# A 128-byte tile at the upper edge of SBUF, in a kernel of linear attention and two MLPs

## The chip, the cores and the metric

The kernel runs on one core of a Trainium2 chip. The metric is the time of one execution on the device in microseconds (us), the median of several runs. The profile is of one execution; its times are counted from the first instruction, and its engines are TensorE (PE for matmuls, PEld for the loading of stationary operands), VectorE (DVE), ScalarE (ACT), GpSimd (POOL) and SyncE (SP).

## The reference

Attention with a feature map makes x of 2304 tokens by 512 features, and two MLPs with different activations follow, all in float32:

```python
q_p, k_p = (phi(q), phi(k))                     # exp(+-proj - max), 256 features
kv = np.einsum('bhsf,bhsd->bhfd', k_p, v)
num = np.einsum('bhsf,bhfd->bhsd', q_p, kv)     # and den; x = num / den
...
h = x @ w_in                                    # 512 -> 2048
g = h * np.cos(h)                               # first MLP
g = np.maximum(h, 0.0) + alpha * np.minimum(h, 0.0)   # second MLP
return (g @ w_out).astype(np.float32)           # 2048 -> 512
```

## The kernel before

**Three products for one.** In the MLPs every operand is split into a high and a low part of type float32r, and a product is the sum of three matmuls, high by high, high by low and low by high. `mm3` (L158 to L164) issues them in this order. All matmuls of both MLPs come from L163.

**A step.** The work of the MLPs is cut into 160 steps: 2 layers, 16 slices of 128 hidden features (`ft`), 5 groups of tokens (four of 512 and one of 256). In `moe_step` a step issues the first matmul of a later step (`hidden`, five steps ahead once the pipeline runs) and the second of its own (`output`), and in between what ACT, DVE and POOL have to do. The order on every engine is the one written out by hand.

- `hidden` is a run of 12 matmuls into a tile `ph`: 4 slices of the 512 features by 3 products. The moving operand is x (`xh`, `xl`), the stationary one is w_in (`wih`, `wil`). The run is 512 columns wide, or 256 in the small group.
- `activate` makes the gated tiles: `gh` is the high part (ACT, L85) and `gl` the low one (POOL, L86) of `r`.
- `output` in the first layer is a run of 12 matmuls into `po`, with the gated tiles as moving operand (512 or 256 columns) and w_out (`woh`, `wol`) as stationary one. In the second layer the roles are exchanged: w_out moves, always 512 columns, and slices of 128 columns of the gated tiles are stationary; a group of 512 tokens gives 12 matmuls, the small one 6.

So of the matmuls at L163 that are 512 columns wide, 1,536 write `ph`, 768 write `po` in the first layer and 864 write `po` in the second. In each layer 48 steps pair a 512-wide `ph` run with a 512-token `po` run, 16 pair a 256-wide `ph` run with a 512-token `po` run, and 16 pair a 512-wide `ph` run with the small group's `po` run, since `ph` is five steps ahead and the small group stays for at most four steps.

**Where the tiles lie.** Pools are taken from the lower end of SBUF upward or, with `side="right"`, from the upper end (229,344 bytes in a partition) downward. On the lower side lie `xh`, `xl`, the tiles of weights, `acc`, and the attention's `wk` and `qpp`; on the upper side lie `gp` (five buffers each of `gh` and `gl`) and `mt` (two of `r`), and before the MLPs the attention's `vp` (v) and `kw` (`kin`, `kp`). A tile of 128 x 512 numbers takes 2048 bytes of a partition. In the kernel before, `xh`, `xl` and all tiles of weights begin at 1888 modulo 2048, and all of `gh`, `gl` and `r` at 2016. Within a tile, the slices of x lie 9216 bytes apart (1024 modulo 2048, so that the four slices begin at 1888 and 864 in turn), and stationary slices of 128 columns lie 512 bytes apart.

Of the kernel before, what the change touches and what calls it, by code (L numbers as in the profile page):

```python
# [10 lines left out]
F32 = mybir.dt.float32  # L11
# [10 lines left out]
P = 128  # L22
# [6 lines left out]
def feature_map_attention_two_mlps(  # L29
# [30 lines left out]

    ctx.enter_context(tc.manual_schedule())

    const = ctx.enter_context(tc.tile_pool(name="const", bufs=1))
    small = ctx.enter_context(tc.tile_pool(name="small", bufs=2))
    xpool = ctx.enter_context(tc.tile_pool(name="xpool", bufs=1))
# [732 lines left out]
```

## Time and profile before

| | |
|---|---|
| time, median of 3 runs | 998.44 us (998.33 to 998.99) |
| profiled execution, first to last instruction (span) | 996.2 us |
| TensorE matmuls busy | 989.7 us, 99% of the span |
| DVE, POOL, ACT busy | 69%, 61%, 50% |
| share of PE in the chain that ended last | 96% |

The span leaves out what lies before the first and after the last instruction; 2.2 us lie between it and the median. No time of its own was taken for the profiled execution, so its span and these 2.2 us stand for it. Matmuls are pipelined: the record of one lasts about 0.39 us, while the next one starts about 0.23 us after it. What a matmul costs is read from start to start, or from a run of them in the chain.

### The profile page before, as it was taken

How to read it: one execution, taken by the hardware profiler on the slowest of the kernel's cores; microseconds unless marked ns; L12 is line 12 of the kernel's file. 1: busy time of each engine (PE TensorE's matmuls, PEld its weight loads, DVE VectorE, ACT ScalarE, POOL GpSimd, SP SyncE). 2: the span in 40 equal slices, each digit the busy share in tenths (PEclk: the TensorE clock that was granted, in tenths of full speed). 3: DMA queues.
4: the chain of work that ended last, by engine and by line, in shares of the span. 5: the costliest groups of instructions: out<-in, count | busy, mean ns of one | idle time of the engine just before them, and what ended most of it. 6: DMA issues, size and time to landing. Idle time of an engine off the chain costs nothing.

```text
span 996.2 us, 13997 instructions
## 1 busy us (share of the span) xinstructions
PE 989.7 (99%) x5145; PEld 838.6 (84%) x5145; DVE 686.3 (69%) x976; ACT 493.9 (50%) x967; POOL 606.4 (61%) x498
## 2 busy tenths in 40 slices
PE   9999999999999999999999999999999999999998
PEld 7999999888888888888888888888888888888886
DVE  6868686668886577647764789587748774875343
ACT  5888888866666476646665663132213221322100
POOL 3577787856667366536655889477537753775221
PEclk9999999999999999999999999999999999999999
DMA  6454543211111021101110111011101110110112
GB/s 166 108 149 120 151 126 91 71 44 60 64 43 64 22 63 44 43 22 62 44 43 22 43 59 48 22 62 45 43 22 58 50 43 22 50 55 1 43 58 91
DMA packets 64580, 60.63 MB, mean 61 GB/s; under 512 B 28928, under 2 KB 54656, under 8 KB 64512
## 3 DMA queue, kind: packets, MB, share of 16 engines
q1 hardware_dynamic: 64512, 59.75, 20.0%
q8 instruction: 40, 0.66, 0.3%
q14 instruction: 28, 0.23, 0.1%
HBM read 52.50 MB, written 4.79 MB: 58 GB/s over the span
## 4 chain that ended last, share of the span: by engine, by line
PE 96%; DVE 1%; ACT 1%; issue 1%; POOL 1%; POOLq 0%; ACTq 0%
PE ph L163 39%; PE po L163 39%; PE pj L453 6%; PE kv L494 5%; PE nm L578 5%; PE tp L534 2%; PE tp L430 0%; DVE acc L243 0%; ACT acc L553 0%; DVE wt L125 0%; DVE wt L122 0%; DVE we L126 0%; ACT qp1h L567 0%; POOL wol L133 0%; POOL gl L86 0%
## 5 line engine op out<-in xcount | busy, mean ns | idle before, releaser
L86 POOL TENSOR_TENSOR gl<-r,gh 128x512 fp32r<-128x512 f32 (+1 forms) x160 | 204.1, 1277 | 305.4 <-ACT gh L85 300.4
L85 ACT CAST gh<-r 128x512 fp32r<-128x512 f32 (+1 forms) x160 | 92.1, 576 | 392.9 <-DVE r L209 266.9
L163 PE MATMUL ph<-xh,wil 128*128 128x512 f32 (+1 forms) x640 | 236.7, 370 | 0.0
L163 PE MATMUL ph<-xh,wih 128*128 128x512 f32 (+1 forms) x640 | 236.5, 370 | 0.0
L163 PE MATMUL ph<-xl,wih 128*128 128x512 f32 (+1 forms) x640 | 236.0, 369 | 0.0
L243 DVE TENSOR_TENSOR acc<-po,acc 128x512 f32<-128x512 f32 (+1 forms) x134 | 86.9, 658 | 104.7 <-PE po L163 104.1
L163 PEld LDWEIGHTS ph<-xl,wih 128*128 128x128 f32 x640 | 120.5, 188 | 22.3 <-POOL xl L622 0.2
L163 PEld LDWEIGHTS ph<-xh,wih 128*128 128x128 f32 x640 | 120.5, 188 | 22.0
L163 PEld LDWEIGHTS ph<-xh,wil 128*128 128x128 f32 x640 | 120.4, 188 | 21.3
L163 PE MATMUL po<-gh,wol 128*128 128x512 f32 (+1 forms) x320 | 119.5, 373 | 0.1
L163 PE MATMUL po<-gh,woh 128*128 128x512 f32 (+1 forms) x320 | 119.0, 372 | 0.0
L163 PE MATMUL po<-gl,woh 128*128 128x512 f32 (+1 forms) x320 | 119.0, 372 | 0.0
L163 PE MATMUL po<-woh,gh 128*128 128x512 f32 x288 | 114.0, 396 | 0.0
L163 PE MATMUL po<-woh,gl 128*128 128x512 f32 x288 | 113.6, 394 | 0.1
L163 PE MATMUL po<-wol,gh 128*128 128x512 f32 x288 | 113.6, 395 | 0.0
L122 DVE SCALAR_TENSOR_TENSOR wt<-ws,we 128x512 int32<-128x512 int32 x64 | 97.9, 1530 | 2.4
L196 DVE TENSOR_SCALAR r<-ph,al 128x512 f32<-128x512 f32 (+1 forms) x80 | 55.3, 691 | 58.0 <-PE ph L163 38.1
L131 POOL TENSOR_TENSOR wu<-wu,we 128x512 f32<-128x512 f32 x64 | 83.0, 1297 | 1.3 <-ACT wu L128 1.3
L207 DVE TENSOR_TENSOR r<-ph,r 128x512 f32<-128x512 f32 (+1 forms) x80 | 50.5, 631 | 47.8 <-ACT r L194 47.7
L569 POOL TENSOR_TENSOR qp1l<-acc,qp1h 128x512 fp32r<-128x512 f32 (+1 forms) x64 | 59.1, 949 | 26.4 <-ACT qp1h L567 26.4
L494 PEld LDWEIGHTS kv<-vm,kp 128*128 128x128 f32 x512 | 72.3, 191 | 2.6 <-ACT qp1h L567 0.4
L494 PE MATMUL kv<-vm,kp 128*128 128x66 f32 x512 | 72.2, 255 | 0.1
(81 smaller groups left out, 1876.0 us busy)
## 6 DMA issues: line engine op xcount, KB each, us to landing
ws<-in_moe_w_in_dram SPq DMA_DIRECT2D x32, 512.0 KB, 3.6
ws<-in_moe_w_out_dram SPq DMA_DIRECT2D x32, 512.0 KB, 3.5
acc<-dr SPq DMA_DIRECT2D x32, 144.0 KB, 3.0
out_dram<-acc SPq DMA_DIRECT2D x18, 256.0 KB, 2.0
vm<-in_v_dram SPq DMA_DIRECT2D x16, 256.0 KB, 3.5
kin<-in_k_dram SPq DMA_DIRECT2D x28, 128.0 KB, 2.8
qin<-in_q_dram SPq DMA_DIRECT2D x28, 128.0 KB, 2.8
acc<-acc SPq DMA_DIRECT2D x16, 144.0 KB, 2.4
```

The costliest lines, as they stand in the source:

```text
L85: nc.scalar.copy(hi, src)
L86: lo_engine.tensor_tensor(out=lo, in0=src, in1=hi.bitcast(F32), op=ALU.subtract)
L122: lambda: stt(out=t, in0=w1, scalar=-0x40000000, in1=e, op0=ALU.bitwise_and, op1=ALU.bitwise_or),
L131: lambda: tt(out=u, in0=u, in1=ef, op=ALU.mult),
L163: nc.tensor.matmul(ps, lhsT=l, rhs=r, start=(first and m == 0), stop=(last and m == n - 1))
L196: nc.vector.tensor_scalar(out=r, in0=ph, scalar1=0.0, scalar2=al[:, ft:ft + 1], op0=ALU.min, op1=ALU.mult)
L207: nc.vector.tensor_tensor(out=r, in0=ph, in1=r, op=ALU.mult)
L243: nc.vector.tensor_tensor(out=a, in0=po, in1=a, op=ALU.add)
L453: nc.tensor.matmul(pj[:, a].rearrange("p j f -> p (j f)"), lhsT=x[:, a * P:(a + 1) * P], rhs=w2.rearrange("p j f -> p (j f)"), start=True, ...
L494: nc.tensor.matmul(ps[:, :, y, :] if pr is None else ps[:, pr, y, :], lhsT=e[:, s, 2 * a + y, :], rhs=vt[:, y] if pr is None else vm[:, pr ...
L569: nc.gpsimd.tensor_tensor(out=dl, in0=et, in1=dh.bitcast(F32), op=ALU.subtract)
L578: nc.tensor.matmul(nm, lhsT=l[:, s, pr, y * VW:(y + 1) * VW], rhs=r[:, s, y, :], start=(s == 0 and m == 0), stop=(s == 1 and m == 2),)
```

## The change

A pool of one tile of 128 x 32 float32 numbers (128 bytes in a partition) is taken at the upper edge of SBUF before any other pool, and no instruction uses it:

```diff
     ctx.enter_context(tc.manual_schedule())
 
+    edge = ctx.enter_context(tc.tile_pool(name="edge", bufs=1, side="right"))
+    edge.tile([P, 32], F32, name="edge")
     const = ctx.enter_context(tc.tile_pool(name="const", bufs=1))
```

All pools of the upper side begin 128 bytes lower: `gh`, `gl` and `r` at 1888 modulo 2048, like x and the weights, and `kin`, `kp` and v 128 bytes below their former places. The lower side stays where it is. No instruction is added, removed or moved.

## Rows read from the trace of the kernel before

**Rows 1.** The page's head and its engines' busy times.
```profile
span 996.2 us, 13997 instructions
...
PE 989.7 (99%) x5145; PEld 838.6 (84%) x5145; DVE 686.3 (69%) x976; ACT 493.9 (50%) x967; POOL 606.4 (61%) x498
```

**Rows 2.** The chain that ended last, by line, from the page.
```profile
PE ph L163 39%; PE po L163 39%; PE pj L453 6%; PE kv L494 5%; PE nm L578 5%; PE tp L534 2%; PE tp L430 0%; DVE acc L243 0%; ACT acc L553 0%; DVE wt L125 0%; DVE wt L122 0%; DVE we L126 0%; ACT qp1h L567 0%; POOL wol L133 0%; POOL gl L86 0%
```

**Rows 3.** Stretches: length, then busy us (count) of each engine, granted clock, DMA.
```profile
560.00:600.00 40.00, 40.00 (x181) 32.81 (x180) 33.67 (x41) 23.34 (x43) 34.61 (x27) 1.00 0.16 54
...
sum 996.20, PE 989.75 PEld 838.65 DVE 686.34 ACT 493.91 POOL 606.43; mean PE 39.59 PEld 33.55 DVE 27.45 ACT 19.76 POOL 24.26
```

**Rows 4.** Groups of instructions by form: one of each kind of 512-wide matmul.
```profile
L163 PE MATMUL ph<-xh,wih 128*128 128x512 f32 x512 | 200.5, 392 | 0.0
...
L163 PE MATMUL po<-woh,gh 128*128 128x512 f32 x288 | 114.0, 396 | 0.0
...
L163 PE MATMUL po<-gh,wol 128*128 128x512 f32 x256 | 101.3, 396 | 0.1
```

**Rows 5.** The chain's pieces at the first step: start, length, what, count.
```profile
196.88 10.90 PE ph L163 x48
```

**Rows 6.** PE in order of time: start and length of two matmuls, twelve apart.
```profile
204.90 0.39 PE L163 MATMUL ph<-xh,wih 128*128 128x512 f32 x1
...
207.62 0.40 PE L163 MATMUL po<-gh,woh 128*128 128x512 f32 x1
```

**Rows 7.** The chain's pieces in the first layer, 512-token groups.
```profile
480.71 2.79 PE po L163 x12
483.50 2.73 PE ph L163 x12
...
508.35 2.79 PE po L163 x12
```

**Rows 8.** The chain's pieces in the second layer, 512-token groups.
```profile
680.53 2.80 PE po L163 x12
683.32 2.76 PE ph L163 x12
...
708.29 2.80 PE po L163 x12
```

**Rows 9.** The chain's pieces in the first layer, `po` runs of the small group.
```profile
448.77 2.76 PE ph L163 x12
451.53 1.44 PE po L163 x12
...
461.37 2.76 PE ph L163 x12
```

**Rows 10.** The chain's pieces in the second layer, `po` runs of the small group.
```profile
648.76 2.73 PE ph L163 x12
651.49 1.40 PE po L163 x6
...
661.14 2.73 PE ph L163 x12
```

**Rows 11.** The chain's pieces near the end, `ph` run of the small group.
```profile
974.91 1.43 PE ph L163 x12
976.35 2.77 PE po L163 x12
...
983.39 4.63 issue
```

**Rows 12.** PE in order of time: the first `po` matmuls of the second layer.
```profile
608.19 0.40 PE L163 MATMUL po<-woh,gh 128*128 128x512 f32 x1
608.43 0.40 PE L163 MATMUL po<-wol,gh 128*128 128x512 f32 x1
```

**Rows 13.** Groups by form: the attention's projections from the lower and the upper side.
```profile
L453 PE MATMUL pj<-w,qin 128*128 128x256 f32 x126 | 33.1, 381 | 0.0
L453 PE MATMUL pj<-w,kin 128*128 128x256 f32 x126 | 33.0, 380 | 0.0
```

## The prediction

> **What bounds the kernel.** I read the page's head first, then the chain, then the stretches. PE is busy for 989.7 of 996.2 us [rows 1], and the chain that ended last runs on PE for 96% of its length, 78% of it in the two kinds of matmul at L163 [rows 2]. [...] So the time is the number of matmuls by the distance from one start to the next, and an edit that adds no instruction can only act through that distance.
>
> A record's length doesn't give it: ph and po records last 392 and 396 ns alike [rows 4], since they overlap. The chain does, because consecutive matmuls of one kind stand in it as one piece. Equal matmuls, 128 x 128 by 512 columns, go at different paces there. Twelve ph matmuls between two starts take 207.62 - 204.90 = 2.72 us [rows 6], and 48 in a row, before any po is mixed in, take 10.90 us, 0.227 us each [rows 5]. Twelve po take 2.79 us in the first layer [rows 7] and 2.80 in the second [rows 8], 0.233 each. The ph runs between them take 2.73 [rows 7] or 2.76 [rows 8]. There is no wait in it: idle time before these groups is 0.0 or 0.1 us in total [rows 4]. It is a pace, and I look for what sets it.
>
> **What differs between ph and po.** While one matmul streams its moving operand, the stationary operand of the next is loaded, so PE reads two places of SBUF at a time (PEld is busy for 84% of the span beside PE's 99% [rows 1]). In ph both places begin at 1888 modulo 2048 plus a multiple of 512 bytes (x at 1888 or 864, slices of w_in 512 apart). In po one of the two is a gated tile at 2016, so they are 128 bytes off that grid, in both layers, though the gated tile moves in the one and is stationary in the other. The slow pace goes with the offset and not with the role. In the twelve ph of rows 6 the four slices put the moving and the next stationary operand at distances of 0, 512, 1024 and 1536 modulo 2048, and none of these four is slower than the other three: 2.72 us over twelve. And ph runs are slower when they lie between po runs (2.73 and 2.76) than when they follow each other (2.72), which I read as a state that the po run leaves behind and that takes some matmuls to die out.
>
> **The change, part by part.** The new tile has no instruction, so it costs nothing by itself, and every engine keeps its program and its order. All of the upper side moves together by 128 bytes, so the tiles that overlap in it (gated tiles over the attention's) are the same ones and no wait between them is new. What is left is the distance between operands on the upper and on the lower side.
>
> *Matmuls at L163.* I take it that po on the grid of 512 goes as ph does, 2.72 us for a run of twelve, and that ph, with nothing off the grid beside it, stays at 2.72. By kinds of step, with the counts of the text above:
> - First layer, 48 full steps: five ph and po pairs take 508.35 - 480.71 = 27.64 us, 5.528 each [rows 7]; at 2 x 2.72 = 5.44 that is 0.088 less, 4.2 us.
> - Second layer, 48 full steps: (708.29 - 680.53) / 5 = 5.552 [rows 8], 0.112 less, 5.4 us.
> - First layer, 16 steps with the small group's po: (461.37 - 448.77) / 3 = 4.20, of which 1.44 are twelve po of 256 columns [rows 9]. Twelve ph of 256 columns take 1.43 [rows 11], so that width gains nothing or 0.01, and the ph run goes from 2.76 to 2.72: 0.04, 0.6 us.
> - Second layer, 16 such steps, with six po of 512 columns: (661.14 - 648.76) / 3 = 4.127 [rows 10]; at 2.72 + 1.36 = 4.08, 0.047 less, 0.75 us.
> - 32 steps with a small ph run and a full po run: 2.79 in the first layer [rows 7], 0.07 less, 1.1 us; 2.77 in the second [rows 11], 0.05 less, 0.8 us.
>
> The sum is 4.2 + 5.4 + 0.6 + 0.75 + 1.1 + 0.8 = 12.85 us.
>
> *What is given back.* A run of another width may leave a state behind too, even on the grid. This happens 48 times (32 small ph runs, 16 small po runs in the first layer). From below it costs nothing; from above it costs 0.04 us, which is what ph pays after a small po run today [rows 9], 1.9 us in all. The nearest row without an offset is the start of ph after the attention's last matmuls, which are of another width: 10.90 against 4 x 2.72 = 10.88, 0.02 us [rows 5]. I take that, 1.0 us. Near the end the chain leaves PE for 4.63 us [rows 11], so some 20 matmuls' gain of 0.006 us is lost, 0.1 us.
>
> *The attention.* kin, kp and v move against the operands of the lower side. The projections read the one (qin) from the lower and the other (kin) from the upper side, at different places modulo 2048, and last 381 and 380 ns [rows 13]: I take 0. For kv and nm, which are mixed matmul by matmul, no row tells; the chain gives them 10% of the span, 100 us [rows 2]. From both sides I allow 1 us, about what 1% of it would be.
>
> *The other engines.* They read and write the tiles at the same distances among themselves, since gh, gl and r move together. Faster steps press them harder: 5.54 to 5.44 us is 2%, so POOL's 34.61 of 40 [rows 3] becomes 88%, still with room. I cost that at nothing; with the room gone, PE would wait for gl, and the gain would shrink, not turn.
>
> So 12.85 - 1.0 - 0.1 = 11.75 us less. The span of 996.2 goes to 984.4 or so, and with the 2.2 us around it, or from the median at once, 998.44 - 11.75 = 986.7 us.
>
> [...]
>
> **The rivals.**
>
> *No change.* The pace follows something that the edit leaves alone. In ph the moving operand changes its place by 1024 from slice to slice and in po it stays in one tile or two, and po goes to other tiles. For it: no po run on the grid is in the trace. Against it: the two layers, with exchanged roles, have the same slow pace, and ph runs suffer from po as neighbours [rows 7, 8]. Time: 998.44, within 1 us by the attention.
>
> *Half of it.* The offset matters, but po on the grid doesn't stay in the even state; each change between ph and po costs as much as today in ph, and all runs take 2.73 to 2.76, 2.745 on average. Then a full pair takes 5.49: 48 x 0.038 + 48 x 0.062 = 4.8 us, and the small steps give some 1.5. Time: 992.1. For it: ph pays that today on either side of po. Against it: 48 ph in a row pay it once at most [rows 5].
>
> *Slower.* The same place modulo 2048 makes the two reads meet, not pass. The first products of every slice 0 have moving and stationary operand at distance 0; if po locks there at the slowest distance that the trace has, 608.43 - 608.19 = 0.24 us [rows 12], the 1,632 po of 512 columns take 0.007 us more each, 11 us. Time: 1009 to 1010. It decides from where a po run of twelve takes over 2.81 us: 2 us over 136 such runs is 0.015 on 2.795. For it: today's offset may be the luckier one of two, and nothing excludes that state for operands fixed in place. Against it: ph has distance 0 in a quarter of its matmuls and goes at 2.72 [rows 6].
>
> **How the numbers follow.** Full gain 0.61, half 0.16, no change 0.15, slower 0.08. The prediction is that of the full gain, 986.7; its own range is 984.7 (nothing given back, and 1 us from the attention) to 989 (all of 1.9 given back, 1 us lost in the attention, and runs at 2.725). The range for 8 in 10 reaches through the half case into the one of no change: 984.7 to 998.5, which leaves out most of the slower case, some of no change and a little below. Faster by over 0.2% (2 us, about what a measurement tells from nothing) is the full and the half case, 0.77; same 0.15; slower 0.08.
>
> **What would show it.** In the chain of the changed kernel, po runs of twelve at 2.72 in both layers, next to ph runs of 2.72; pairs of 5.44. Half the gain would show as 2.73 to 2.76 in both kinds. If po stays at 2.79 and 2.80, the place isn't the cause. If po takes 2.83 or more, they meet. If PE shows waits for gl or gh that aren't there now, another engine took over. I would be wrong most simply if the grid is not 512 bytes wide where one operand lies at the upper end of SBUF, which no row shows.

## The result and the profile after

987.69 us median (987.54 to 987.93) against 998.38 for the kernel before on the same chip: a ratio of 0.9888, 95% interval 0.9877 to 0.9900, 10.7 us less. Forecast were 986.7 us, 984.7 to 989 for the full gain and 984.7 to 998.5 for the range as a whole.

The page's head, against [rows 1]: the same instructions and a span 10.2 us shorter. PE's busy time is 11.6 us less (989.7 to 978.1), so PE is idle for 1.4 us more than before.

```profile
span 986.0 us, 13997 instructions
...
PE 978.1 (99%) x5145; PEld 838.0 (85%) x5145; DVE 688.5 (70%) x976; ACT 493.9 (50%) x967; POOL 606.5 (62%) x498
```

The chain's pieces of the changed kernel in the first layer (start, length, what, count), two line numbers further down than before. They answer to [rows 7].

```profile
481.27 2.72 PE ph L165 x12
483.99 2.72 PE po L165 x12
486.71 2.72 PE ph L165 x12
```

And in the second layer, against [rows 8]:

```profile
678.31 2.72 PE ph L165 x12
681.03 2.72 PE po L165 x12
683.75 2.72 PE ph L165 x12
```

Where 2.79 and 2.80 alternated with 2.73 and 2.76, every run of twelve beside others of its width takes 2.72, in both layers and in both kinds. A pair went from 5.53 and 5.55 to 5.44. The runs that are not at 2.72 stand behind a run of another width. In the chain, first the first layer, then the second, against [rows 9 to 11]:

```profile
449.69 1.43 PE po L165 x12
451.12 2.75 PE ph L165 x12
```
```profile
630.61 1.43 PE ph L165 x12
632.04 2.75 PE po L165 x12
...
642.95 1.36 PE po L165 x6
644.31 2.72 PE ph L165 x12
```

After twelve matmuls of 256 columns, the next run of 512 columns takes 2.75; after six po of 512 columns, it takes 2.72. PE in order of time shows where the 0.03 us go in such a run:

```profile
446.78 0.40 PE L165 MATMUL ph<-xh,wih 128*128 128x512 f32 x1
...
448.17 0.39 PE L165 MATMUL ph<-xh,wih 128*128 128x512 f32 x1
...
449.53 0.28 PE L165 MATMUL po<-gh,woh 128*128 128x256 f32 x1
```

The first six take 448.17 - 446.78 = 1.39 us, the last six 449.53 - 448.17 = 1.36, which is 0.227 each. So what the change of width leaves behind is gone after six matmuls when the operands are on the grid.

PE's waits on POOL in the changed kernel (waited for: us in total, times, longest us). In the kernel before, PE's matmuls have none, though its weight loads wait at the same two places:

```profile
PE ph L165 <- POOL xl L624: 0.3, 1, 0.3
PE po L165 <- POOL wol L135: 0.2, 1, 0.2
```

The weight loads there, before and after:

```profile
PEld po L163 <- POOL wol L133: 0.5, 1, 0.5
...
PEld ph L163 <- POOL xl L622: 0.2, 1, 0.2
```
```profile
PEld po L165 <- POOL wol L135: 0.7, 1, 0.7
PEld ph L165 <- POOL xl L624: 0.6, 1, 0.6
```

### The profile page after: what moved, and what is told of

Read it like the earlier page. It is cut to its first block, busy times and chain, and to the rows that moved or that the text cites. A ratio compares the mean times of both kernels' runs of the same rounds, so it can differ in the third digit from the quotient of the medians.

```text
span 986.0 us, 13997 instructions
## 1 busy us (share of the span) xinstructions
PE 978.1 (99%) x5145; PEld 838.0 (85%) x5145; DVE 688.5 (70%) x976; ACT 493.9 (50%) x967; POOL 606.5 (62%) x498
## 4 chain that ended last, share of the span: by engine, by line
PE 94%; ACT 2%; DVE 1%; issue 1%; DMA 1%; POOL 1%; SPq 0%; POOLq 0%; ACTq 0%
PE po L165 39%; PE ph L165 38%; PE pj L455 6%; PE kv L496 5%; PE nm L580 5%; PE tp L536 2%; DMA acc<-in_q_dram 0%; DMA dn<-acc 0%; ACT acc L555 0%; DVE r L192 0%; DVE wt L127 0%; ACT acc L593 0%; ACT r L195 0%; ACT r L184 0%; ACT r L196 0%
```

## The experiments

All place tiles of no use, as the change does, and nothing else, but for three that also shift x within a longer tile. "Distance" is the place of the moving operand minus that of the stationary operand of the next matmul, modulo 256, where all slices of x, of the weights and of the gated tiles fall together. The chain's pieces are given as above.

**Place or distance.** The tile at the lower end instead of the upper (x and weights join the gated tiles at 2016):

```diff
+    low = ctx.enter_context(tc.tile_pool(name="low", bufs=1))
+    low.tile([P, 32], F32, name="low")
     const = ctx.enter_context(tc.tile_pool(name="const", bufs=1))
```

> The tile of 128 bytes lies at the lower end instead of the upper: x and the weights go up to 2016 modulo 2048 and meet the gated tiles, which stay at 2016. If the distance between the two operands counts (my theory): as the changed kernel, 987.7 us, all runs of twelve at 2.72. If the place of the gated tiles itself counts (rival: 1888 is good, 2016 is bad at the upper end): as before, 998.4, po at 2.79 and 2.80.

Measured: 987.50 us, ratio 0.9896 (0.9882 to 0.9911), all runs of twelve beside others of their width at 2.72. Then the tile at both ends, this one and that of the change:

> A tile of 128 bytes at either end: the gated tiles lie at 1888 as in the changed kernel, x and the weights at 2016, so the distance of 128 bytes is back with the other sign. Distance theory: slow again, 998 us within 3, po at 2.77 to 2.83. Rival of the gated tiles' own place: 987.7, po at 2.72.

Measured: 998.67 us, ratio 1.0003 (0.9994 to 1.0013). The gated tiles lie where the changed kernel has them, and the slow pace is back; the second layer in the chain:

```profile
680.98 2.80 PE po L167 x12
683.78 2.76 PE ph L167 x12
```

So the distance counts and not the gated tiles' own place, and +128 and -128 go alike, po at 2.79 in the first layer and 2.80 in the second for both (with the period of 256 found below they are one and the same distance).

**The slow pace handed to ph.** The tile between x and the weights (x at 1888, everything else at 2016), none at the upper edge:

```diff
     xpool = ctx.enter_context(tc.tile_pool(name="xpool", bufs=1))
+    low = ctx.enter_context(tc.tile_pool(name="low", bufs=1))
+    low.tile([P, 32], F32, name="low")
```

> A tile of 128 bytes between x and the weights on the lower side, none at the upper edge: weights and gated tiles at 2016, x alone at 1888. Distance theory: po goes at 2.72 or is held up a little by its neighbours (up to 2.76), and ph takes over the slow pace, 2.77 to 2.83; 128 ph runs by 0.075 and 136 po runs by up to 0.025 make 9.6 to 13 us over the changed kernel, 997 to 1000 us. Rival that the slow pace is po's own (other tiles, the high part taken twice in a row from one place): po stays at 2.79 to 2.80 and ph gets no slower than 2.76.

Measured: 997.91 us, ratio 0.9998 (0.9988 to 1.0008). The total alone would say that nothing happened. The chain says that the two kinds changed places:

```profile
484.40 2.79 PE ph L165 x12
487.19 2.73 PE po L165 x12
489.93 2.79 PE ph L165 x12
```

The pace isn't po's own. The run on the grid takes 2.73 beside a neighbour off it, as ph did in the first layer before the change.

**The same place modulo what.** The upper tile with 640 bytes instead of 128, so that the gated tiles lie 512 bytes below the weights modulo 2048:

> The upper tile has 640 bytes instead of 128, so the gated tiles begin at 1376 modulo 2048, 512 bytes below the weights and x. If the grid is 512 bytes (my theory): 987.7 us, all runs at 2.72. If the same place modulo 2048 is what counts (rival): po slower than 2.73, the time above 989 and up to 998.

Measured: 987.75 us, ratio 0.9897 (0.9883 to 0.9912), all full runs at 2.72. The same place modulo 2048 isn't needed.

**Other distances.** The next runs change two sizes, the lower tile's (between x and the weights) and the upper one's. Here 256 and 1856 bytes:

```diff
+    edge = ctx.enter_context(tc.tile_pool(name="edge", bufs=1, side="right"))
+    edge.tile([P, 464], F32, name="edge")
...
+    low = ctx.enter_context(tc.tile_pool(name="low", bufs=1))
+    low.tile([P, 64], F32, name="low")
```

> Other distances modulo 2048: ph at 256 (weights 256 bytes above x), po at 64. Both signs of 128 gave the same sequence of paces, so I expect a period of 256: ph has its pace of 2.72 when it follows ph and 2.72 to 2.76 beside po. If the period is 512 (rival), ph at 256 differs from 2.72 also in the middle of a run. For po at 64: half way between 0 and 128 gives 2.755 and with ph at 2.735 about 994 us; a pace as even as at 0 gives 988.

Measured: 998.38 us, ratio 0.9998 (0.9989 to 1.0007); neither 994 nor 988. Pieces of the first layer, then of the second:

```profile
480.85 2.76 PE po L167 x12
483.62 2.77 PE ph L167 x12
```
```profile
680.68 2.80 PE po L167 x12
683.48 2.75 PE ph L167 x12
```

po differs by layer. The gated tiles lie 64 above the weights; in the first layer they move (distance +64, 2.76), in the second they are stationary (-64, 2.80). I had left the sign out. Lower 64 and upper 1856 bytes:

> The two distances exchanged: ph at 64, po at 256. Period of 256: po 2.72 to 2.76; ph at 64 as po was in the run with po at 64, since moving and stationary operands count alike. Time within 1.5 us of that run, since there are 128 runs of the one and 136 of the other. If po differs from ph at the same distance, the role or the tile counts after all (rival).

Measured: 997.53 us, ratio 0.9990 (0.9981 to 1.0000), 0.9 from the run before. ph, now at -64, takes 2.80, as po of the second layer did there. po at 256, in the chain and then matmul by matmul:

```profile
481.11 2.74 PE po L167 x12
483.85 2.80 PE ph L167 x12
```
```profile
480.94 0.39 PE L167 MATMUL po<-gh,woh 128*128 128x512 f32 x1
...
482.32 0.39 PE L167 MATMUL po<-gh,woh 128*128 128x512 f32 x1
...
483.68 0.39 PE L167 MATMUL ph<-xh,wih 128*128 128x512 f32 x1
```

Its first six matmuls take 1.38 us and its last six 1.36, the pace of the grid. So the grid is 256 bytes wide and not 512. Lower 32 bytes, no upper tile:

> Distances of 32 (ph) and 96 (po), no tile at the upper edge. If the pace grows with the distance from the grid, ph is near 2.74 and po near 2.78, 995 us. If it depends on whether both fall into one line of 64 or 128 bytes (rival), 32 is as 0 (2.72) or 96 is as 128 (2.79), in steps and not in proportion.

Measured: 1006.34 us, ratio 1.0078 (1.0063 to 1.0093), slower than before and 11 us above what I had. po at +96 and -96 takes 2.81, ph at -32 2.79 to 2.80. Nothing grows in proportion with the distance. Lower 192 and upper 1824 bytes:

> Distances of 192 (ph) and 160 (po), on the other side of 128. If the sign doesn't count (period 256), 192 is as 64 and 160 as 96 in the two runs before, run of twelve by run of twelve within 0.01 us. If it counts (rival), they differ; a distance at which a run takes under 2.72 would show here or in the three before.

Measured: 1000.30 us, ratio 1.0020 (1.0011 to 1.0030). The weights lie 192 above x, so ph's distance is -192, which is +64 modulo 256, and po's is -96 in the first layer and +96 in the second. First layer:

```profile
487.10 2.81 PE po L167 x12
489.92 2.75 PE ph L167 x12
```

The expectation that the sign doesn't count fell: 192 isn't as 64 in the run before (2.80). It is as +64 in the run with po at 64 (2.76): the period of 256 holds, with the sign.

**How exact it must be.** x was put 16, -16 and 8 bytes off by a slice in a longer tile (from number 4, 60 or 2 on; 60 numbers are 240 bytes, -16 modulo 256; the weights go up by 512 bytes and stay on the grid); the first kernel also has an upper tile of 96 bytes, the others of 128:

```diff
-    xh = xpool.tile([P, KD, NTOK], F32R, name="xh")
-    xl = xpool.tile([P, KD, NTOK], F32R, name="xl")
+    xh, xl = (
+        xpool.tile([P, KD * NTOK + 64], F32R, name=nm)[:, 4:4 + KD * NTOK].rearrange(
+            "p (k n) -> p k n", k=KD
+        )
+        for nm in ("xh", "xl")
+    )
```

> By the runs so far the pace depends on the moving operand's place minus that of the next stationary one, with its sign, modulo 256. Here that distance is +16 in ph, +32 in po of the first layer and -32 in po of the second. My theory from the earlier runs: the second layer's po at 2.79 to 2.80, as ph was at -32; +32 lies between 0 (2.72) and +64 (2.76) and gives up to 2.80; +16 at 2.72 if one line of 32 or 64 bytes is what has to agree, 2.75 or more if every byte counts (rival). 990 to 1000 us.

Measured: 1002.40 us, ratio 1.0034 (1.0021 to 1.0047); ph 2.78, po 2.80 in both layers. The time lies above the 990 to 1000 that I had: +16 isn't on the grid, and +32 is as slow as -32.

> ph at -16, po on the grid. If -16 is as slow as -32, ph at 2.79 and po at 2.74 beside it, 997 us; if it is within one line with 0, 987.7. A pace under 2.72 in the middle of a run would be new.

Measured: 997.61 us, ratio 0.9988 (0.9979 to 0.9997); ph 2.80, but po 2.72 beside it, where I had 2.74.

> ph at +8, po on the grid. If lines of 16 bytes or more are what count, as the changed kernel, 987.7 us and 2.72 everywhere; if every byte counts (rival), ph over 2.74 and 991 us or more.

Measured: 1000.95 us, ratio 1.0020 (1.0010 to 1.0030). Eight bytes are as bad as 128, and po on the grid beside them takes 2.75, where it took 2.73 with x 128 bytes off:

```profile
485.66 2.81 PE ph L169 x12
488.47 2.75 PE po L169 x12
```

**The MLPs' part alone.** The tile is taken when the attention's pools of the upper side are given back, so kin, kp and v stay where they were:

```diff
                 pctx.close()
+                edge = ctx.enter_context(tc.tile_pool(name="edge", bufs=1, side="right"))
+                edge.tile([P, 32], F32, name="edge")
                 pools["gp"]
```

> The tile of 128 bytes is taken only when the attention's upper pools are given back, so gh, gl and r move to 1888 as in the changed kernel while kin, kp and v stay where they were before. If the attention's places cost nothing (my prediction's step): 987.7 us within 0.5, all runs of the MLPs at 2.72. If moving them gave or took something (rival), the time differs from 987.7 by that, up to 1 us either way.

Measured: 987.53 us, ratio 0.9891 (0.9874 to 0.9907), all full runs at 2.72. The median is 0.2 from the changed kernel's, within the noise. The spans tell more: 984.9 to 985.5 us in its four executions, 985.8 to 986.0 in the changed kernel's four. So the attention's places do cost something; how much is worked out below.

## Why the prediction was right

**The bound.** PE's pace sets the time: the MLPs became shorter by the distance between starts (twelve po of 512 columns from 2.79 and 2.80 to 2.72), with the same 13,997 instructions.

**The cause.** The step from the rows to "128 bytes off the grid" held, and the rivals fell each on its own run. *No change*: exchanging which operand is off exchanges which run is slow. *Half of it*: all runs beside others of the same width are at 2.72, none at 2.73 to 2.76. *Slower*: distance 0 is not the slow one; for 512 columns, of the eleven distances tried (0, +8, +16, +32, +64, +96, 128, -96, -64, -32, -16) it has the best pace, 0.227 us, and 2.75 to 2.82 for twelve, beside runs of the same width, were measured at the others. The grid was called 512 bytes; it is 256, which changes nothing in the sum, since 128 is off both.

**The sum.** The full pairs came out as put down, 5.44 in both layers. In the MLPs, from the first ph run to the end, the stretch went from 996.2 - 188.19 = 808.0 to 986.0 - 188.86 = 797.1 us: 10.9 less, where 12.85 - 1.1 = 11.75 was forecast. The chains there: before, after, and in the kernel that leaves the attention's tiles in place:

```profile
188.19 2.77 PE ph L163 x12
```
```profile
188.86 2.75 PE ph L165 x12
```
```profile
188.23 2.76 PE ph L163 x12
```

Two terms of the MLPs were sized too small. What a change of width leaves behind is 0.027 us and not 0.02 (2.747 against 2.720, medians by the starts in the trace), 48 times 1.3 instead of 1.0 us. And "I cost that at nothing", of the other engines, left out that two weight loads already waited for POOL, for `xl` and for `wol`; these waits grew. The run of twelve at the first goes from 1.66 to 2.04 us, the one at the second from 3.10 to 3.31, though its pace alone makes it 0.05 shorter: 0.6 us together. With 0.1 for the end, which no run read by itself, that is 12.85 - 1.3 - 0.6 - 0.1 = 10.85. The chain shows the first of the two waits:

```profile
211.21 1.44 POOL xl L624
212.69 0.50 PE ph L165 x2
```

Only at the second does the faster pace explain the wait: counted from the first ph run, PE is there 1.2 us earlier and `wol` only 1.0. At the first PE is 0.1 earlier, and `xl`, of the attention's end, comes 0.3 later; why it does isn't traced. POOL was forecast at 88% of its fullest stretch and is at 36.22 of 40, 91%; PE's matmuls wait for it at these two places alone.

```profile
560.00:600.00 40.00, 40.00 (x178) 33.10 (x177) 33.15 (x39) 22.64 (x42) 36.22 (x28) 1.00 0.17 54
```

Two slips of the working change little. In the second layer the small group's last four steps have no ph run beside them, so there are 12 such steps and not 16 (under 0.1 us). And the upper end of the range for the full gain, with the terms named there, is 986.7 + 0.9 + 1 + 264 x 0.005 = 989.9, not 989.

**The attention** was taken at 0, with 1 us allowed either way, and that term was wrong by some 0.7 us. The first ph run of the changed kernel begins 0.67 us later than before, and only 0.04 later where kin, kp and v stay in place (lines above). It isn't the load of q, for which PE waits 1.2 us in the one trace and 1.1 in the other. From start to start, the 917 matmuls of kv and nm that are followed by another of them take 105.63 us before and 105.55 with the tiles in place, but 106.06 in the changed kernel. With a tile at both ends, where the two sides lie as before modulo 256, they take 105.52; in the seven kernels where the sides are 128 off their former distance, 106.03 to 106.13. So these matmuls too pay for places, 0.4 us of it here; the rest of the 0.7 isn't traced.

The span thus fell by 10.9 - 0.7 = 10.2 us, to 986.0, where the working has 984.4. That the median is only 1.0 above the forecast is in part luck: outside the span of the profiled execution lie 1.8 us (987.77 in all) and not the 2.2 taken over from before.

**What stays open.** Twelve matmuls of one form took from 2.72 us (the changed kernel) to 2.82 (first layer, lower 192 and upper 1824 bytes) by the operands' places alone. By what means the places act was not shown: the runs give paces for distances. Nor is it settled whether the matmul's own stationary operand or the next one's counts: within a run both lie on the same grid. The last ph matmul before a po run of the second layer, where they differ, takes 0.232 us before the change against 0.227 in the first layer, but with the gated tiles 64 bytes off 0.226 against 0.227. Why 0.227 us is the best pace is open as well.

## What to carry to other kernels

Where PE is the bound and equal matmuls go at different paces, compare the places of their moving and stationary operands before looking for a wait: in these kernels float32r matmuls of 512 columns were fastest where the moving and the stationary operand agree modulo 256 bytes, 2.72 us for twelve against 2.75 to 2.82 at the ten other distances, and 8 bytes off already took 2.81. Move only what has to move: shifting the attention along with the gated tiles cost 0.7 us of the gain. Read the pace from runs in the chain, not from the records' lengths (392 and 396 ns hid all of it), and look at both kinds of run: a total that doesn't move can hide a loss of one and a gain of the other.

## What was not expected of the hardware

Eight bytes off cost as much as 128: 2.81 against 2.79 and 2.80 for twelve matmuls. The sign counts: +64 takes 2.75 to 2.76 and -64 takes 2.80. The disturbance is often carried on: a run on the grid takes up to 2.77 after one that is off it or of another width (ph at 256 beside po at +64), and in the kernel before it goes back to 0.227 us a matmul after one to nine. But not always: after ph at -16, po on the grid takes 2.72.

And the grid is the best place for 512 columns, not for 256. Twelve matmuls of 256 columns take 1.43 us on it, and ph at +64 takes 1.41 in the second layer and 1.36 in the first (the run with lower 192 and upper 1824 bytes):

```profile
322.80 1.36 PE ph L167 x12
```
